# Finishing of a chunk's value sums, spread over more places of the loop

## The chip, the cores and the metric

The kernel runs on one core of one Trainium2 chip. The metric is the device time of one execution in microseconds (us). Engines are named as the profile names them: PE is TensorE (PEld its weight loads), DVE is VectorE, ACT is ScalarE, POOL is GpSimd, SP is SyncE.

## The reference: what is computed

For one sequence of 2048 rows and 512 features in float32 the result is `g * a + (1 - g) * b`. `g` is a sigmoid of a row sum. `b` is a SwiGLU network with 1792 hidden features. `a` is attention with 32 heads of 16 features in a sliding window of 256 keys:

```
scores = einsum("bhqd,bhkd->bhqk", q, k) * Dh ** -0.5
mask   = (i - j >= 0) & (i - j < 256)
p      = softmax(where(mask, scores, -1e9))
o      = einsum("bhqk,bhkd->bhqd", p, v)
a      = o.reshape(B, S, D) @ wo
```

The change lies in the last step of `o`: the sums over the keys are divided by the softmax's denominators and stored.

## The kernel before, in words

The 32 heads are worked on in 8 groups of four. A group's 2048 queries are 16 blocks of 128, and four blocks make a chunk of 512 queries. So there are 32 chunks in all.

The order of the work is written out by hand. The main loop, from L698, counts `t` from 0 to 128. Each `t` is one block of one group and has four steps, `hd` = 0 to 3, one for each head. Four values of `t`, `part` = 0 to 3, make a **slot** `d`: sixteen steps, one chunk. A pair (part, hd) names a step of a slot, and this document writes it (0,0) to (3,3). Engines take their instructions in the order in which the loop writes them, each engine in its own queue, and the framework adds a wait wherever one instruction touches data that another still uses.

Each step writes, in this order:

- `stage1` (L302, L304) for the next group: PE multiplies queries and keys into a PSUM tile `ps` of the pool `ps1`, and DVE adds the mask and takes the row maximum. The pool has two buffers, so the matmul of a step needs the DVE result of two steps before. The last group has no next group, so from t = 112 on there is no `stage1`.
- `stage2` (L344, L346, L348, L351) for this group: PE computes the transposed scores, ACT takes the exponential into `pt`, and POOL cuts two masks into `pt` once in two steps, at hd = 1 and hd = 3.
- three pairs of matmuls (L252) of the gate, up or projection products, which fill PE between the two stages.
- the functions put down in `AT` for this step, such as evictions, products, splits into high and low parts (`split`, L73, whose low part POOL computes) and DMAs.
- at some steps, one piece of `FIN`.

At (0,1), after everything else of the step, `av` (L356) writes the value products of the chunk that the previous slot has made ready: some 2 us of matmuls (L368) in which PE does nothing else. It leaves two PSUM tiles, `first` and `second`. The generator `finish` (L375) then turns them into stored results, one piece at each `run(FIN, 1)`. It uses two SBUF tiles of 128x512, `o0` and `o1`, which are called `both` and `ot` for even chunks; for odd chunks the names are swapped (L381). The pieces before the change, with the steps at which they are written:

- (0,1): ACT copies `second` to `both` (L383).
- (0,2): DVE adds `first` (L385, and L387 for a group's first chunk).
- (1,1): DVE transposes `both` into `ot` in 32x32 blocks (L389).
- (1,3): DVE takes the reciprocal of the denominators (L393) and multiplies all 512 columns' sums by it (L394).
- (2,1): DVE transposes `ot` back into `both` (L397), and POOL issues the DMA that stores `both` in `od` (L398).

After the loop the last phase begins: four matmul tiles of the SwiGLU part (L770), then the products with `wo`, which read `od`, and the down projection.

Of the kernel before, what the change touches and what calls it, by code (L numbers as in the profile page):

```python
# [12 lines left out]
ALU = mybir.AluOpType  # L13
# [3 lines left out]
P = 128  # L17
S, D, H, DH, W, F = 2048, 512, 32, 16, 256, 1792
NK = D // P
NB = S // P  # L20
CH = 512
# [15 lines left out]
def gated_mix(ctx, tc, xT, xn, wqk, wv, wo, wgu, wd, gw, outT):  # L37
# [4 lines left out]
    nc = tc.nc  # L42
# [51 lines left out]
    def run(gen, n=None):  # L94

        while n is None or n > 0:
            if next(gen, run) is run:
                break
            n = n and n - 1
# [101 lines left out]
    with ExitStack() as A:  # L201
# [88 lines left out]
        def stage1(g, qb):  # L290

            hf, b = divmod(qb, NB // 2)
            if b == 0:
                MX[g, hf] = sm.tile([P, 4, NB // 2], F32, name="mx")
            q0, k0 = qb * P, max(0, qb - 2) * P
            n = q0 + P - k0
            for hd in range(4):
                pr, j = divmod(hd, 2)
                r = slice(64 * j, 64 * j + 63)

                ps = ps2.tile([P, CH], F32, name="ps2") if g == 0 and pr else ps1.tile([P, CH], F32, name="ps1")
                nc.tensor.matmul(ps[:, :n], QT[g % 2][pr][r, q0:q0 + P], KT[g % 2][pr][r, k0:k0 + n],  # L302
                                 start=True, stop=True)
                mx = nc.vector.tensor_tensor_reduce(out=ps[:, :n], in0=ps[:, :n], in1=mask[:, 3 * P - n:],  # L304
                                                    scale=1.0, scalar=NEG, op0=ALU.add, op1=ALU.max,
                                                    accum_out=MX[g, hf][:, hd, b:b + 1])
                if g == 0:
                    BEHIND.append(mx)
                yield
# [18 lines left out]
        def load_v(n):  # L328

            VG[n] = sm.tile([P, 4, VW], F32, name="vg", bufs=4)  # L330
            nc.sync.dma_start(VG[n], vd[n // 4, :, n % 4 * 4:n % 4 * 4 + 4])

        def stage2(g, kb):


            n = min(3, NB - kb) * P
            k0 = kb * P
            for hd in (1, 0, 3, 2):
                pr, j = divmod(hd, 2)
                r = slice(64 * j, 64 * j + 64)  # L340
                if j:
                    pt = PT[g, kb, pr] = ptp.tile([P, 2, 3 * P], F32, name="pt")
                ps = ps2.tile([P, CH], F32, name="ps2")
                nc.tensor.matmul(ps[:, :n], KT[g % 2][pr][r, k0:k0 + P], QT[g % 2][pr][r, k0:k0 + n],  # L344
                                 start=True, stop=True)
                BEHIND.append(nc.scalar.activation(pt[:, j, :n], ps[:, :n], AF.Exp, scale=SCALE))  # L346
                if not j:
                    nc.gpsimd.affine_select(out=pt[:, :, :P], in_=pt[:, :, :P], pattern=[[0, 2], [1, P]],  # L348
                                            compare_op=ALU.is_ge, fill=0.0, base=0, channel_multiplier=-1)
                    if n == 3 * P:  # L350
                        nc.gpsimd.affine_select(out=pt[:, :, 2 * P:], in_=pt[:, :, 2 * P:],  # L351
                                                pattern=[[0, 2], [-1, P]], compare_op=ALU.is_ge, fill=0.0,
                                                base=-1, channel_multiplier=1)
                yield

        def av(g, c):  # L356


            AV[g, c] = (pp.tile([P, CH], F32, name="pb" if 4 * g + c + 1 < G * NB // 4 else "pa"),
                        ps1.tile([P, CH], F32, name="ps1") if 4 * g + c + 1 >= 4 * (G - 1) else ps2.tile([P, CH], F32, name="ps2"))  # L360

            todo = [(h, 4 * c + m) for h, m in SEQUENCE if 4 * c + m >= 0]
            at = [[n for n, (o, _) in enumerate(todo) if o == h] for h in range(2)]
            for n, (h, kb) in enumerate(todo):
                o, k0 = HALVES[h], kb * P + 64 * h
                q0, q1 = max(k0, c * CH), min(k0 + W + 64, c * CH + CH)
                for j in range(4):
                    nc.tensor.matmul(AV[g, c][h][32 * j:32 * j + 32, q0 - c * CH:q1 - c * CH],  # L368
                                     VG[4 * g + kb // 4][o, kb % 4, 17 * j:17 * j + 32],
                                     PT[g, kb, j // 2][o, j % 2, q0 - kb * P:q1 - kb * P],  # L370
                                     start=n == at[h][0], stop=n == at[h][-1], skip_group_check=True)
# [3 lines left out]
        def finish(g, c):  # L375


            first, second = AV[g, c]
            if not AB:
                AB.extend(osb.tile([P, CH], F32, name=f"o{n}") for n in range(2))  # L380
            both, ot = AB[::-1] if c % 2 else AB  # L381
            lo = 0 if c else 64
            nc.scalar.copy(both[:, lo:], second[:, lo:])  # L383
            yield
            nc.vector.tensor_tensor(out=both[:, lo:], in0=first[:, lo:], in1=both[:, lo:], op=ALU.add)  # L385
            if lo:
                nc.vector.tensor_copy(both[:, :lo], first[:, :lo])  # L387
            yield
            nc.vector.transpose(ot, both)  # L389
            yield  # L390
            v = ot.rearrange("p (s e) -> p s e", e=32)
            rc = osb.tile([P, CH // 32], F32, name="rc")
            nc.vector.reciprocal(rc, v[:, :, DH])  # L393
            nc.vector.tensor_tensor(out=v[:, :, :DH], in0=v[:, :, :DH],  # L394
                                    in1=rc[:, :, None].to_broadcast([P, CH // 32, DH]), op=ALU.mult)
            yield
            nc.vector.transpose(both, ot)  # L397
            nc.gpsimd.dma_start(od[g, :, c * CH:(c + 1) * CH], both)  # L398
            yield

# [142 lines left out]
        def later(t, hd, *fs):  # L543
            AT.setdefault((t, hd), []).extend(fs)
# [65 lines left out]
        def unit(t):  # L610

            def both(n, name):
                key, hf = TURNS[t // 2 + n]
                done = (group_half(t, key[1], hf) if key[0] == "p" else (gate_half, up_half)[key[2]](t, key[1], hf))
                two = []

                def turn(m):
                    if not two:
                        two.extend(lanes(pp, name, [products(key, 2 * hf + m) for m in range(2)], done))
                    yield from two[m]  # L620
                return turn(0), turn(1)
            (a0, a1), (b0, b1) = (both(n, name) for n, name in enumerate(("pa", "pb")))
            return [a0, b0, a1, b1]
# [55 lines left out]
        for b in range(NB):  # L679
            t, hd = blocks[b]  # L680
            later(t, hd, lambda b=b: gate_block(b))
            if b > 1:
                t, hd = blocks[b - 2]
# [10 lines left out]

        FIN = iter(())
        for t in range(G * NB + 1):  # L698
            g, i = divmod(t, NB)
            d, part = divmod(t, NSLOT)  # L700
            if part == 0:
                turns = unit(t) if t < G * NB else [iter(())] * NSLOT
            s1 = stage1(g + 1, i) if t < g7 else iter(())
            s2 = stage2(g, i) if t < G * NB else iter(())
            for hd in range(4):
                run(s1, 1)
                if t < g7:
                    run(s2, 1)
                elif hd % 2 == 0:
                    run(s2, 2)  # L710
                run(turns[part], 3)
                for f in AT.pop((t, hd), ()):
                    f()
                if (part, hd) in ((0, 2), (1, 1), (1, 3), (2, 1)):
                    run(FIN, 1)
                if hd == 1 and part == 0:
                    if t:
                        ag, c = divmod(d - 1, NCH)
                        av(ag, c)
                        FIN = finish(ag, c)  # L720
                        run(FIN, 1)
            if i in (7, 15) and g + 1 < G:
                later(t + 1, 2, lambda g=g, i=i: put_max(g + 1, i // 8))
            if t >= 10 and t % 4 == 2 and t + 6 < G * NB:
                load_v((t + 6) // 4)
        run(FIN)
        for key in sorted(AT):
# [4 lines left out]
    with ExitStack() as B:  # L732
# [7 lines left out]
        def column():  # L740
            return hp.tile([P, CH], F32, name="sg", bufs=4)
# [321 lines left out]
        two, t, part, rest = bank(4, 1), *(column() for _ in range(3))  # L1063
# [46 lines left out]
```

## Time and profile before

| | |
|---|---|
| median of three runs | 805.55 us (805.36 to 805.84) |
| the profiled execution's own time | 804.89 us |
| its span, first to last instruction | 803.2 us |
| busy: PE, PEld | 797.1 us (99%), 688.1 us (86%) |
| busy: DVE, ACT, POOL | 627.8 us (78%), 433.0 us (54%), 345.4 us (43%) |
| mean granted clock of TensorE | 0.999 |

The profile is of one execution. Its instructions are counted from the start of the span. Idle time of an engine ahead of a group of instructions is given with what ended it; a name such as "DVE mx L304" is the instruction that released the waiting one. The main loop's slots run from about 79 us to about 601 us, some 16.3 us each.

### The profile page before, as it was taken

What the parts mean: (1) busy time and instruction counts of PE and PEld (TensorE: products, weight loads), DVE (VectorE), ACT (ScalarE), POOL (GpSimd) and SP (SyncE); (2) the same over time, 40 slices, a digit from 0 to 9 for tenths busy, and PEclk for the clock granted to TensorE, in tenths of its full rate; (3) what the DMA queues carried; (4) which work ended last, traced back from release to release, by engine and by line L of the source; (5) the groups of instructions that cost most, each with busy time, mean ns of one, the idle gap of its engine ahead of it and who ended that gap; (6) DMA issues with size and microseconds to landing.
All of it is one profiled execution on the core that took longest, in us unless ns stands there. A gap on an engine that the chain in (4) does not pass through costs nothing.

```text
span 803.2 us, 21509 instructions
## 1 busy us (share of the span) xinstructions
PE 797.1 (99%) x8247; PEld 688.1 (86%) x8247; DVE 627.8 (78%) x1686; ACT 433.0 (54%) x883; POOL 345.4 (43%) x647
## 2 busy tenths in 40 slices
PE   9999999999999999999999999999999999999998
PEld 7888999889889889889988988888888888888886
DVE  6397787868887787878777878888675478899896
ACT  7412656665566566555666656645643235554642
POOL 7711546564545556544656454546740111000212
PEclk9999999999999999999999999999999999999999
DMA  8574514424252453351444516335637899728436
GB/s 300 168 219 144 141 68 131 128 97 143 68 159 78 117 167 97 114 159 53 138 115 129 151 44 201 130 102 173 202 100 234 263 345 316 292 62 272 93 53 105
DMA packets 62107, 121.88 MB, mean 152 GB/s; under 512 B 10868, under 2 KB 19828, under 8 KB 61748
## 3 DMA queue, kind: packets, MB, share of 16 engines
q1 hardware_dynamic: 54900, 99.27, 39.9%
q0 software_dynamic: 7104, 21.24, 9.0%
q8 instruction: 65, 1.06, 0.6%
q14 instruction: 38, 0.31, 0.1%
HBM read 55.97 MB, written 39.34 MB: 119 GB/s over the span
## 4 chain that ended last, share of the span: by engine, by line
PE 97%; DVE 2%; DMA 0%; SPq 0%; issue 0%; ACT 0%
PE pa L252 24%; PE pb L252 24%; PE ps L302 6%; PE ps L368 5%; PE ps L344 4%; PE ps L89 4%; PE ps L88 4%; PE ps L90 4%; PE pb L368 4%; PE pb L232 2%; PE pa L232 2%; PE pb L89 2%; PE pb L88 2%; PE pa L89 2%; PE pa L88 2%; PE pb L90 2%
## 5 line engine op out<-in xcount | busy, mean ns | idle before, releaser
L304 DVE CUSTOM_DVE_ANT_0 ps<-ps,mask 128x384 f32<-128x384 f32 (+2 forms) x512 | 268.7, 540 | 100.2 <-PE ps L344 51.1
L346 ACT ACTIVATE pt<-ps 128x384 f32<-128x384 f32 (+2 forms) x512 | 238.5, 475 | 130.7 <-PE ps L302 74.0
L348 POOL TENSOR_SCALAR_AFFINE_SELECT pt<-pt 128x256 f32<-128x256 f32 x256 | 108.4, 424 | 200.5 <-ACT pt L346 199.7
L344 PE MATMUL ps<-q,k 64*128 64x384 f32 (+2 forms) x512 | 161.7, 333 | 0.0
L302 PE MATMUL ps<-k,q 63*128 63x384 f32 (+2 forms) x512 | 159.6, 332 | 0.5 <-DVE mx L304 0.5
L252 PE MATMUL pb<-xhi,wh 64*128 64x512 f32 x512 | 116.7, 395 | 0.0
L252 PE MATMUL pb<-xlo,wh 64*128 64x512 f32 x512 | 115.3, 391 | 0.0
L252 PE MATMUL pb<-xhi,wl 64*128 64x512 f32 x512 | 115.2, 391 | 0.0
L252 PE MATMUL pa<-xhi,wh 64*128 64x512 f32 x512 | 113.9, 393 | 0.0
L252 PE MATMUL pa<-xlo,wh 64*128 64x512 f32 x512 | 112.8, 391 | 0.0
L252 PE MATMUL pa<-xhi,wl 64*128 64x512 f32 x512 | 112.6, 391 | 0.0
L302 PEld LDWEIGHTS ps<-k,q 63*128 63x128 f32 x512 | 88.7, 185 | 16.9 <-DVE mx L304 3.6
L351 POOL TENSOR_SCALAR_AFFINE_SELECT pt<-pt 128x256 f32<-128x256 f32 x224 | 100.3, 448 | 0.0
L344 PEld LDWEIGHTS ps<-q,k 64*128 64x128 f32 x512 | 90.8, 184 | 3.6 <-ACT pt L346 0.2
L368 PE MATMUL ps<-pt,vg 64*32 64x320 f32 (+4 forms) x1408 | 74.2, 346 | 0.0
L304 DVE DVE_READ_ACCUMULATOR2_ANT mx<- 128x1 f32 x512 | 71.6, 140 | 0.0
L368 PE MATMUL pb<-pt,vg 64*32 64x320 f32 (+2 forms) x1360 | 69.9, 349 | 0.0
L252 PEld LDWEIGHTS pb<-xhi,wh 64*128 64x128 f32 x512 | 61.6, 185 | 6.0 <-DVE o L385 0.4
L252 PEld LDWEIGHTS pb<-xhi,wl 64*128 64x128 f32 x512 | 61.8, 184 | 5.1
L252 PEld LDWEIGHTS pa<-xhi,wl 64*128 64x128 f32 x512 | 59.4, 184 | 5.9
L252 PEld LDWEIGHTS pa<-xhi,wh 64*128 64x128 f32 x512 | 59.7, 186 | 3.8
L252 PEld LDWEIGHTS pb<-xlo,wh 64*128 64x128 f32 x512 | 61.9, 185 | 0.3
(305 smaller groups left out, 1612.5 us busy)
## 6 DMA issues: line engine op xcount, KB each, us to landing
kept_h<-ev SPq DMA_DIRECT2D x52, 256.0 KB
od<-o POOLq DMA_DIRECT2D x32, 256.0 KB, 3.7
raw<-wgu SPq DMA_DIRECT2D x28, 256.0 KB
q<-xhi SPq DMA_DIRECT2D x56, 128.0 KB
k<-xhi SPq DMA_DIRECT2D x56, 128.0 KB
outT<-sg POOLq DMA_DIRECT2D x28, 256.0 KB, 4.5
vd<-vs POOLq DMA_DIRECT2D x8, 672.0 KB, 4.8
vg<-vd SPq DMA_DIRECT2D x32, 168.0 KB
```

Of the source, the lines that this page charges most:

```text
L88: nc.tensor.matmul(ps, lh, rh, start=start and i == 0, stop=False, skip_group_check=skip)
L89: nc.tensor.matmul(ps, lh, rl, start=False, stop=False, skip_group_check=skip)
L90: nc.tensor.matmul(ps, ll, rh, start=False, stop=stop and i == n - 1, skip_group_check=skip)
L232: nc.tensor.matmul(ps, w, x, start=n == 0, stop=n == len(todo) - 1)
L252: mm = nc.tensor.matmul(ps[me], w[r], x[r], start=not second and i == 0, stop=bool(second) and i == n - 1)
L302: nc.tensor.matmul(ps[:, :n], QT[g % 2][pr][r, q0:q0 + P], KT[g % 2][pr][r, k0:k0 + n], start=True, stop=True)
L304: mx = nc.vector.tensor_tensor_reduce(out=ps[:, :n], in0=ps[:, :n], in1=mask[:, 3 * P - n:], scale=1.0, scalar=NEG, op0=ALU.add, op1=ALU.m ...
L344: nc.tensor.matmul(ps[:, :n], KT[g % 2][pr][r, k0:k0 + P], QT[g % 2][pr][r, k0:k0 + n], start=True, stop=True)
L346: BEHIND.append(nc.scalar.activation(pt[:, j, :n], ps[:, :n], AF.Exp, scale=SCALE))
L348: nc.gpsimd.affine_select(out=pt[:, :, :P], in_=pt[:, :, :P], pattern=[[0, 2], [1, P]], compare_op=ALU.is_ge, fill=0.0, base=0, channel_mu ...
L351: nc.gpsimd.affine_select(out=pt[:, :, 2 * P:], in_=pt[:, :, 2 * P:], pattern=[[0, 2], [-1, P]], compare_op=ALU.is_ge, fill=0.0, base=-1, ...
L368: nc.tensor.matmul(AV[g, c][h][32 * j:32 * j + 32, q0 - c * CH:q1 - c * CH], VG[4 * g + kb // 4][o, kb % 4, 17 * j:17 * j + 32], PT[g, kb, ...
```

## The change

The reciprocal stays at (1,3), alone. The multiplication is cut into two halves of 256 columns each, at (2,0) and (2,2). The second transposition moves to (0,1) of the next slot, behind that slot's `av`, and the DMA that stores the chunk moves to (0,3) of the next slot. A second generator, `OLD`, holds the rest of the previous chunk's `finish` for this. At steps where both stand, `FIN` now comes ahead of the functions of `AT`, and `OLD` at (0,3) comes behind them. The tiles `o0` and `o1` and their swap are the same.

```
             nc.vector.reciprocal(rc, v[:, :, DH])
-            nc.vector.tensor_tensor(out=v[:, :, :DH], in0=v[:, :, :DH],
-                                    in1=rc[:, :, None].to_broadcast([P, CH // 32, DH]), op=ALU.mult)
             yield
+            for s in (slice(0, CH // 64), slice(CH // 64, CH // 32)):
+                nc.vector.tensor_tensor(out=v[:, s, :DH], in0=v[:, s, :DH],
+                                        in1=rc[:, s, None].to_broadcast([P, CH // 64, DH]), op=ALU.mult)
+                yield
             nc.vector.transpose(both, ot)
+            yield
             nc.gpsimd.dma_start(od[g, :, c * CH:(c + 1) * CH], both)
             yield
...
-        FIN = iter(())
+        FIN = OLD = iter(())
...
                 run(turns[part], 3)
+                if (part, hd) in ((0, 2), (1, 1), (1, 3), (2, 0), (2, 2)):
+                    run(FIN, 1)
                 for f in AT.pop((t, hd), ()):
                     f()
-                if (part, hd) in ((0, 2), (1, 1), (1, 3), (2, 1)):
-                    run(FIN, 1)
+                if (part, hd) == (0, 3):
+                    run(OLD)
                 if hd == 1 and part == 0:
                     if t:
                         ag, c = divmod(d - 1, NCH)
                         av(ag, c)
-                        FIN = finish(ag, c)
+                        OLD, FIN = FIN, finish(ag, c)
+                        run(OLD, 1)
                         run(FIN, 1)
```

## The prediction

> **What bounds the kernel now.** I read the page's busy times first, then what PE waits for, then the order of events on DVE, POOL and PE around one chunk's finishing.
>
> ```profile
> PE 797.1 (99%) x8247; PEld 688.1 (86%) x8247; DVE 627.8 (78%) x1686; ACT 433.0 (54%) x883; POOL 345.4 (43%) x647
> ```
>
> PE is the bound: 797.1 of 803.2 us. DVE matters only where it makes PE wait, and that is at the mask-and-maximum, L304. The groups of line 302, its matmul, say how much that costs today.
>
> ```profile
>   DVE mx L304: 4.1, 13
> ```
>
> PE stood idle ahead of L302 for 4.1 us in 13 places. That is the most that a smoother DVE could give back through this wait. The clearest place lies in the slot that begins at 191.4 us (timelines of DVE, POOL, PEld and PE):
>
> ```profile
> 201.35 1.15 DVE L394 TENSOR_TENSOR o<-o,rc 128x256 f32<-128x256 f32 x1
> 202.90 0.13 DVE L304 DVE_READ_ACCUMULATOR2_ANT mx<- 128x1 f32 x1
> ...
> 200.93 1.29 POOL L73 TENSOR_TENSOR xlo<-ev,xhi 128x512 fp32r<-128x512 f32 x1
> ...
> 203.09 0.18 PEld L302 LDWEIGHTS ps<-k,q 63*128 63x128 f32 x1 [0.66 <-DVE mx L304]
> ...
> 201.14 0.45 PE L252 MATMUL pa<-xhi,wh 64*128 64x512 f32 x2
> 202.00 0.40 PE L252 MATMUL pa<-xhi,wh 64*128 64x512 f32 x2
> 203.31 0.45 PE L252 MATMUL pa<-xhi,wh 64*128 64x512 f32 x2
> ```
>
> The multiplication takes 1.15 us there, while a POOL subtraction runs beside it. The maximum comes late, the weight load of L302 waits 0.66 us, and the step from 202.00 to 203.31 takes 1.31 us where the one before it took 0.86. So such a collision costs PE about 0.45 us. The rows also give two latencies that I need below: L304's last part ended at 203.03, the weight load started 0.06 us later, and the step's L252 came 0.22 us after that.
>
> **The change part by part.** One whole chunk in the middle shows what is there:
>
> ```profile
> 314.13 0.71 DVE L389 STREAM_TRANSPOSE o<-o 128x512 f32<-128x512 f32 x1
> 314.76 0.53 DVE L304 CUSTOM_DVE_ANT_0 ps<-ps,mask 128x384 f32<-128x384 f32 x1
> 315.21 0.13 DVE L304 DVE_READ_ACCUMULATOR2_ANT mx<- 128x1 f32 x1
> ...
> 315.87 0.25 DVE L393 RECIPROCAL rc<-o 128x16 f32<-128x16 f32 x1
> 316.15 0.51 DVE L394 TENSOR_TENSOR o<-o,rc 128x256 f32<-128x256 f32 x1
> ...
> 310.83 0.57 DVE L304 CUSTOM_DVE_ANT_0 ps<-ps,mask 128x384 f32<-128x384 f32 x1 [2.86 <-PE ps L344]
> ...
> 318.61 0.56 POOL L398 DMA_DIRECT2D od<-o  x1
> ```
>
> *The multiplication in halves.* The 0.51 us at (1,3) becomes two instructions at (2,0) and (2,2). The trace has no half; each costs between 0.25 and 0.51 us, and I take 0.3. Both lie beside PE's step of 0.87 us. If that cover were gone, they would add 0.1 us to a slot. The gain is bounded by 0 and the 4.1 us above. I count two collisions like the one shown, 0.9 us.
>
> *The second transposition at (0,1).* It costs the same 0.71 us, but DVE stands idle for 2.86 us there, while PE does the value products. It is free, and ACT's copy L383 behind it waits for those products anyway.
>
> *The DMA at (0,3) of the next slot.* This is the part that costs. In the code of before, chunk c stores from `both`, and chunk c+1 uses that same tile as its `ot`: the first transposition L389 overwrites it. So L389 must wait until the store of the chunk before has landed. Today the store is issued at 318.61 and the next L389 comes 13 steps later, some 12 us. After the change the store is written at (0,3) and L389 at (1,1), two steps later. How long a store takes (groups of line 398, issue to landing):
>
> ```profile
> L398 POOL DMA_DIRECT2D od<-o x32: 560/560/584, 105.0 to 604.8; - x32
> ...
> DMA to landing us min/median/max: 2.3/3.7/7.7
> ```
>
> No store of 32 landed in less than 2.3 us, and two steps are 1.75 us. Queued behind L389 on DVE is L304 of step (1,2), for which L302 of step (2,0) waits, and with it all of PE. I work it out at three of the slots, the first that is hit, one in the middle, and the last. The rows are POOL's last mask cut of step (0,3), behind which the store will stand; L389; the end of L304 of step (1,2); and PE's first L252 of step (2,0). For the middle slot the second and third stand above.
>
> ```profile
> 115.95 0.41 POOL L351 TENSOR_SCALAR_AFFINE_SELECT pt<-pt 128x256 f32<-128x256 f32 x1
> ...
> 117.53 0.71 DVE L389 STREAM_TRANSPOSE o<-o 128x512 f32<-128x512 f32 x1
> ...
> 118.61 0.14 DVE L304 DVE_READ_ACCUMULATOR2_ANT mx<- 128x1 f32 x1
> ...
> 119.11 0.45 PE L252 MATMUL pa<-xhi,wh 64*128 64x512 f32 x2
> ...
> 312.83 0.41 POOL L351 TENSOR_SCALAR_AFFINE_SELECT pt<-pt 128x256 f32<-128x256 f32 x1
> ...
> 315.88 0.39 PE L252 MATMUL pa<-xhi,wh 64*128 64x512 f32 x1
> ...
> 526.89 0.41 POOL L351 TENSOR_SCALAR_AFFINE_SELECT pt<-pt 128x256 f32<-128x256 f32 x1
> ...
> 528.10 0.71 DVE L389 STREAM_TRANSPOSE o<-o 128x512 f32<-128x512 f32 x1
> ...
> 529.19 0.13 DVE L304 DVE_READ_ACCUMULATOR2_ANT mx<- 128x1 f32 x1
> ...
> 529.97 0.44 PE L252 MATMUL pa<-xhi,wh 64*128 64x512 f32 x2
> ```
>
> Middle slot: the cut ends at 313.24, the store is issued at about 313.27 and lands 2.3 us later at 315.57 at best. L389 starts 0.06 us after that, at 315.63 instead of 314.13, so 1.50 us late. L304 then ends at 316.84 instead of 315.34, and the L252 follows 0.06 + 0.22 us behind, at 317.12 instead of 315.88: PE loses 1.24 us. In the same way the first slot loses 1.14 us and the last 1.21. The mean is 1.2 us with a store at its fastest; every further microsecond of the store is one more for PE.
>
> *How many slots.* The first chunk has no store ahead of it. The slots of the last group have no L304 that could hold PE:
>
> ```profile
> L304 DVE CUSTOM_DVE_ANT_0 ps<-ps,mask x512: 288/566/601, 37.6 to 536.8; 128x384 f32<-128x384 f32 x150, 128x128 f32<-128x128 f32 x11, 128x256 f32<-128x256 f32 x10
> ```
>
> Its last instruction stands at 536.8 us, so 26 of the 32 transpositions count, those from 117.53 to 528.10. 26 x 1.2 = **31.2 us**. The other five I take at nothing, since PE's matmuls of the same slots cover the late DVE work; without that cover they would cost 5 x 1.2 = 6 us.
>
> *Whether the store has the DMA engines to itself.* For each of the 26 slots I took the stretch in which the new store would move its bytes, 1.1 to 2.0 us after its issue, and read the share of the DMA engines that other transfers take there today. In 16 of them it is 0.11 or less, in 10 it is 0.24 to 1.00. The first and the last of either kind:
>
> ```profile
> 117.49:118.39 0.90, 0.90 (x12) 0.90 (x10) 0.90 (x4) 0.49 (x1) 0.70 (x2) 1.00 0.03 9
> 528.43:529.33 0.90, 0.90 (x12) 0.76 (x10) 0.90 (x4) 0.49 (x1) 0.61 (x2) 1.00 0.00 0
> ...
> 134.22:135.12 0.90, 0.90 (x12) 0.78 (x10) 0.86 (x4) 0.52 (x2) 0.51 (x2) 1.00 0.78 191
> 494.88:495.78 0.90, 0.90 (x12) 0.85 (x10) 0.89 (x3) 0.49 (x1) 0.62 (x2) 1.00 1.00 370
> ```
>
> A free store takes 2.3 us. For a shared one I take 3.0, half way to the median of 3.7: 10 x 0.7 = **7.0 us**. The bounds are 0 (all at 2.3) and 26 x 1.4 = 36.4 us (all at the median).
>
> The Trainium skill gives a formula in its page "DMA: Bandwidth & Descriptors", section "Anatomy of one DMA — SWDGE (gpsimd) path": about 2.0 us fixed and the bytes at 436 GB/s. An estimate by it is 2.6 us for 256 KB; all 26 slots at that would add 26 x 0.3 = 8 us to the 31.2 in place of my 7.0. The row's least value lies below it and its median above, so the trace agrees only between the two.
>
> *What stands ahead of the store on POOL.* At (0,3) the functions of `AT` come first. In three slots one of them is a POOL subtraction of an `xlo`, which today follows right behind the last mask cut of (0,3):
>
> ```profile
> 198.44 1.81 POOL L73 TENSOR_TENSOR xlo<-ev,xhi 128x512 fp32r<-128x512 f32 x1
> ...
> 329.84 1.80 POOL L73 TENSOR_TENSOR xlo<-ev,xhi 128x512 fp32r<-128x512 f32 x1
> ...
> 461.28 1.30 POOL L73 TENSOR_TENSOR xlo<-ev,xhi 128x512 fp32r<-128x512 f32 x1
> ```
>
> It delays the store by its own length. I take the shorter, 1.3 us, because DVE will be waiting beside it: 3 x 1.3 = **3.9 us**. POOL itself, past which the DMA moves, gains nothing for PE: its mask cuts now stand behind an issue at (0,3) instead of (2,1), 0.56 us either way, while POOL has idle time in every slot.
>
> *The end.* The last chunk's transposition waits for the store of the one before it, at most some 3 us. PE then works on four SwiGLU tiles that need nothing of it. I take 0, with 3 us as the bound.
>
> The sum: 31.2 + 7.0 + 3.9 - 0.9 = 41.2 us. Against the profiled execution's own time that is 804.89 + 41.2 = 846.1 us. The median of the runs lies 0.66 us above the profiled execution, so I forecast 847 us.
>
> **The rivals.**
>
> *The store lands in time.* This is the case that isn't slower. If a store landed within about 1.1 us of its issue (2.3 less the 1.2 us that PE loses), or if L389 had nothing to wait for, PE would lose nothing and keep the gain: 804.9 - 0.9 = 804.0, down to 800.8 with all of the 4.1 us. Against it stands the least landing of 2.3 us in 32, and that the two tiles alternate by chunk and no third one is added. Chance 0.03.
>
> *PE's clock falls while it waits.* The end of the trace shows that an idle PE loses its clock (stretches of time, granted clock in the column after POOL):
>
> ```profile
> 799.00:800.00 1.00, 0.18 (x2) 0.00 (x0) 0.96 (x3) 0.00 (x0) 0.00 (x0) 1.00 0.64 250
> ...
> 801.00:802.00 1.00, 0.00 (x0) 0.00 (x0) 0.00 (x0) 0.00 (x0) 0.00 (x0) 0.90 0.36 124
> 802.00:803.20 1.20, 0.00 (x0) 0.00 (x0) 0.00 (x0) 0.00 (x0) 0.00 (x0) 0.50 0.00 0
> ```
>
> PE's last matmul ends near 799.2, and the clock goes to 0.50 near 801.8, 2.6 us later. Stalls of 1.2 us repeated once a slot are shorter, but those behind a shared store or a POOL subtraction come near. If each stall cost as long at half clock as the fall took, 2.6 us, PE would lose 1.3 us more in each: 26 x 1.3 = 34, and the time would be 881 us. Chance 0.05. The Trainium skill's page "TensorE: Matmul & The Clock Gate", section on the HAM clock gate, says that the clock halves after an idle window of about 3.4 us and returns after as long a busy one; an estimate by that page is 1.7 us a stall and 891 us if every stall triggered it, and nothing if none does, since none of mine is that long. The 2.6 us of the trace are in its range, since the page lets the windows run free.
>
> *Every store is shared.* The stores now all leave at one place of the slot, and the SP queue's transfers may move towards them as the slots get longer. Then all 26 take the median: 31.2 + 36.4 + 3.9 - 0.9 = 70.6, 876 us. For it speaks the median of today; against it the 16 free stretches. Chance 0.10.
>
> *PE loses only half.* If in a stalled slot POOL's mask cut of (0,3) came earlier against DVE, the stall would shrink; at half of it the time is 804.9 + 20.6 = 826 us. Against it: POOL's cuts follow ACT's exponentials, which follow PE, and so does L389. Chance 0.05.
>
> **How the numbers follow.** My forecast has 0.76. The five chances leave 0.01 for anything else. A change of under 0.2% can't be told from none here. Slower by more is every case but the first: 0.96. Faster by over 0.2% needs more than 1.6 us of gain with no stall: 0.02. Within: 0.02. The range runs from 828 us (all stores at 2.3 us, no delay on POOL, all of the 4.1 us gained is 832, and some of the half-loss case) to 877 us (every store at the median). It leaves out the clock, the landing in time and half of the half loss, about 0.12.
>
> **What would show it.** On DVE, idle time ahead of L389 with the store as its releaser, 1.5 us or more in each of the 26 slots; PE idle ahead of L302 of step (2,0), released by L304, some 40 us in all; the steps (2,0) 1.2 us longer. The transposition L397 in DVE's gap during the value products, with no wait behind it. The 0.45 us losses behind L394 gone. I am wrong if L389 starts on time, if PE's loss sits elsewhere, or if the granted clock falls below 0.99.

## The result

The changed kernel takes 864.92 us (863.69 to 866.82, four runs); the kernel before took 805.45 us in the same comparison (805.11 to 805.84). The ratio is 1.074, with a 95% interval of 1.073 to 1.075. So it is 59.5 us slower. The forecast was 847 us, in a range of 828 to 877: the direction and the wait behind it hold, the size came out 18 us larger, and a second mechanism, PE's clock, took a part that the forecast had put at nothing. The figures of the experiments below leave out one execution of 1119.07 us, in which the granted clock was 0.655.

The page of the changed kernel, busy times, and two of its costliest groups (busy, mean ns of one, then idle time ahead of the group and what ended it):

```profile
PE 818.0 (95%) x8247; PEld 694.5 (80%) x8247; DVE 632.0 (73%) x1718; ACT 432.2 (50%) x883; POOL 337.9 (39%) x647
...
L302 PE MATMUL ps<-k,q 63*128 63x384 f32 (+2 forms) x512 | 165.0, 342 | 39.9 <-DVE mx L304 39.9
...
L389 DVE STREAM_TRANSPOSE o<-o 128x512 f32<-128x512 f32 x32 | 22.8, 711 | 57.8 <-DMA od<-o 57.8
```

Before, PE was busy for 99% of its span; now it is 95% of a longer one. DVE stands idle for 57.8 us ahead of L389, always until a store of `od` has landed, where before it never waited there. PE stands idle for 39.9 us ahead of L302 until DVE's maximum L304.

The slot that the prediction worked out in the middle of the loop now looks like this (timelines of DVE, POOL, PEld and PE):

```profile
340.34 0.14 DVE L304 DVE_READ_ACCUMULATOR2_ANT mx<- 128x1 f32 x1
342.39 0.71 DVE L389 STREAM_TRANSPOSE o<-o 128x512 f32<-128x512 f32 x1 [1.91 <-DMA od<-o]
343.02 0.53 DVE L304 CUSTOM_DVE_ANT_0 ps<-ps,mask 128x384 f32<-128x384 f32 x1
343.48 0.13 DVE L304 DVE_READ_ACCUMULATOR2_ANT mx<- 128x1 f32 x1
...
339.58 0.56 POOL L401 DMA_DIRECT2D od<-o  x1
...
343.66 0.18 PEld L302 LDWEIGHTS ps<-k,q 63*128 63x128 f32 x1 [1.84 <-DVE mx L304]
...
341.39 0.41 PE L252 MATMUL pb<-xhi,wh 64*128 64x512 f32 x2
343.95 0.39 PE L252 MATMUL pa<-xhi,wh 64*128 64x512 f32 x2
```

The store is issued at 339.58, behind the mask cuts of step (0,3). DVE is done with step (1,1) at 340.48 and waits 1.91 us, until 342.39. L304 of step (1,2) ends at 343.61, the weight load of L302 follows 0.05 us later, and PE's step from 341.39 to 343.95 takes 2.56 us instead of 0.87. This is the chain that the prediction wrote down, instruction by instruction; only this slot's store took 2.8 us and not 2.3.

Where the 61.9 us between the two profiled spans went, from the starts of PE's steps in the two traces:

| part | us |
|---|---|
| the loop's first slot begins later | 1.0 |
| step (1,3) of the slots 2 to 27, behind L389 | 47.6 |
| steps behind it in the same slots, at half clock | 11.2 |
| other differences of these slots, the collisions' gain among them | -1.3 |
| last group, slots 28 to 30 | 3.3 |

The second part was forecast as 31.2 + 7.0 + 3.9 = 42.1 us. The third stood only in a rival. It is seen best in one slot (stretches of time, their length, the busy time of PE, PEld, DVE, ACT and POOL, then the granted clock, the DMA share and GB/s), and in PE's first L252 of its next steps:

```profile
241.80:245.20 3.40, 3.40 (x36) 2.92 (x34) 2.82 (x9) 1.93 (x4) 2.02 (x5) 1.00 0.33 131
245.20:248.60 3.40, 0.98 (x10) 0.50 (x6) 0.67 (x2) 0.53 (x2) 0.76 (x2) 1.00 0.42 134
248.60:252.00 3.40, 2.80 (x14) 2.69 (x16) 2.34 (x10) 0.86 (x2) 0.00 (x0) 0.51 0.00 0
252.00:255.50 3.50, 3.50 (x20) 3.31 (x20) 1.61 (x7) 1.10 (x3) 0.82 (x3) 0.51 0.00 0
255.50:258.90 3.40, 3.40 (x34) 3.30 (x32) 2.89 (x9) 2.88 (x7) 1.69 (x3) 1.00 0.00 0
...
249.69 0.70 PE L252 MATMUL pa<-xhi,wh 64*128 64x512 f32 x2
251.29 0.70 PE L252 MATMUL pa<-xhi,wh 64*128 64x512 f32 x2
```

From 245.2 to 248.6 PE works for 0.98 us of 3.40, and then the clock is half until 255.5. The steps take 1.60 us (249.69 to 251.29) instead of 0.87. The slots 2 to 27 have seven such falls, five of 3.4 us and two of 6.8 us, 30.7 us in all; one more lies in the last group.

The Trainium skill, page "TensorE: Matmul & The Clock Gate", section "Part 1: The HAM clock gate (the "warmup" mystery)", describes a free-running window of about 3.4 us; the distances between the falls in this trace are whole multiples of 3.41 us, so that agrees. It says that the clock halves after an idle window. Here a part of a window was enough: ahead of the seven falls PE stood idle for 1.91 to 2.75 us of the window, and no window of the slots 2 to 27 with 1.73 us or less began one.

### The profile page after: what moved, and what is told of

Read it like the earlier page. It is cut to its first block, busy times and chain, and to the rows that moved or that the text cites. A ratio compares the mean times of both kernels' runs of the same rounds, so it can differ in the third digit from the quotient of the medians.

```text
span 865.1 us, 21536 instructions
## 1 busy us (share of the span) xinstructions
PE 818.0 (95%) x8247; PEld 694.5 (80%) x8247; DVE 632.0 (73%) x1718; ACT 432.2 (50%) x883; POOL 337.9 (39%) x647
## 4 chain that ended last, share of the span: by engine, by line
PE 77%; DMA 10%; DVE 4%; POOL 3%; ACT 3%; issue 2%; SPq 0%; POOLq 0%; ACTq 0%; DVEq 0%
PE pa L252 21%; PE pb L252 14%; DMA od<-o 8%; PE ps L302 6%; PE ps L368 4%; PE ps L88 4%; PE ps L89 4%; PE ps L90 4%; PE pb L368 3%; PE ps L344 3%; DVE o L389 2%; ACT pt L346 2%; PE pb L232 2%; PE pa L89 2%; PE pb L88 2%
## 5 line engine op out<-in xcount | busy, mean ns | idle before, releaser
L304 DVE CUSTOM_DVE_ANT_0 ps<-ps,mask 128x384 f32<-128x384 f32 (+2 forms) x512 | 269.9, 542 | 105.6 <-PE ps L302 55.7
L348 POOL TENSOR_SCALAR_AFFINE_SELECT pt<-pt 128x256 f32<-128x256 f32 x256 | 107.7, 421 | 267.6 <-ACT pt L346 267.1
L302 PE MATMUL ps<-k,q 63*128 63x384 f32 (+2 forms) x512 | 165.0, 342 | 39.9 <-DVE mx L304 39.9
L344 PE MATMUL ps<-q,k 64*128 64x384 f32 (+2 forms) x512 | 167.1, 344 | 1.4 <-ACT pt L346 1.4
L302 PEld LDWEIGHTS ps<-k,q 63*128 63x128 f32 x512 | 91.3, 190 | 65.2 <-DVE mx L304 52.2
L252 PE MATMUL pa<-xhi,wh 64*128 64x512 f32 x512 | 115.4, 411 | 0.0
L252 PE MATMUL pa<-xlo,wh 64*128 64x512 f32 x512 | 114.2, 408 | 0.0
L252 PE MATMUL pa<-xhi,wl 64*128 64x512 f32 x512 | 113.6, 406 | 0.0
L252 PE MATMUL pb<-xhi,wh 64*128 64x512 f32 x512 | 110.5, 394 | 0.0
L252 PE MATMUL pb<-xlo,wh 64*128 64x512 f32 x512 | 109.1, 391 | 0.0
L252 PE MATMUL pb<-xhi,wl 64*128 64x512 f32 x512 | 109.1, 391 | 0.0
L344 PEld LDWEIGHTS ps<-q,k 64*128 64x128 f32 x512 | 93.7, 189 | 7.1 <-ACT pt L346 2.7
L351 POOL TENSOR_SCALAR_AFFINE_SELECT pt<-pt 128x256 f32<-128x256 f32 x224 | 93.8, 419 | 0.0
L304 DVE DVE_READ_ACCUMULATOR2_ANT mx<- 128x1 f32 x512 | 71.9, 140 | 0.0
L389 DVE STREAM_TRANSPOSE o<-o 128x512 f32<-128x512 f32 x32 | 22.8, 711 | 57.8 <-DMA od<-o 57.8
L252 PEld LDWEIGHTS pa<-xhi,wl 64*128 64x128 f32 x512 | 59.3, 195 | 6.7
L252 PEld LDWEIGHTS pa<-xhi,wh 64*128 64x128 f32 x512 | 59.0, 195 | 4.1
L252 PEld LDWEIGHTS pb<-xhi,wh 64*128 64x128 f32 x512 | 56.0, 186 | 5.9
L252 PEld LDWEIGHTS pb<-xhi,wl 64*128 64x128 f32 x512 | 56.0, 184 | 5.9
```

Of the source, the lines that this page charges most:

```text
L252: mm = nc.tensor.matmul(ps[me], w[r], x[r], start=not second and i == 0, stop=bool(second) and i == n - 1)
```

## The experiments

Each kernel is given as a diff against the changed kernel, unless the text says otherwise; `...` marks lines left out.

### The store two written steps earlier

```
-            yield
             nc.gpsimd.dma_start(od[g, :, c * CH:(c + 1) * CH], both)
```

> The changed kernel with one yield taken out: the store of a chunk is issued at (0,1), right behind the transposition L397, and not two written steps later at (0,3). Everything else is as changed. Theory (the whole loss is L389 waiting at (1,1) for that store, and what PE and its clock lose by it): the store now has the value products' 2.2 us more, lands near 311 in a slot where L389 starts at 314, the wait vanishes, the granted clock is 0.998 or more, and the time is 804 us (803 to 806). Rival (the transposition at (0,1), the halves, or the new order against the other functions of a step cost something of their own): it stays above 815 us with DVE or ACT as the releaser.

Measured: 815.09 us, ratio 1.0125 (1.0102 to 1.0149), granted clock 0.999. Idle time ahead of L389, and ahead of L302 (here the waits of its weight load, 11.8 us, and of its matmul, 7.2 us, are added):

```profile
  DMA od<-o: 17.1, 12
...
  DVE mx L304: 18.9, 22
```

One line takes 50 of the 59.5 us away, but not all of it, so the number was missed by 11 us. L389 still waits in 12 slots, longest 5.4 us (after the loop's last chunk, where it holds no L304). In those of the slots 2 to 27 the store landed only 3.5 to 6.0 us after its issue, and in four of them it also left some 3 us behind the transposition, because POOL had mask cuts and subtractions (L73) to do first; step (1,3) still loses 9.6 us over the slots 2 to 27. The releaser is the same store, not DVE or ACT as the rival had it.

### The store alone moved

The diff is against the kernel before.

```
             nc.vector.transpose(both, ot)
+            yield
             nc.gpsimd.dma_start(od[g, :, c * CH:(c + 1) * CH], both)
...
+                if (part, hd) == (0, 3):
+                    run(OLD)
...
-                        FIN = finish(ag, c)
+                        OLD, FIN = FIN, finish(ag, c)
```

> The kernel before with one part of the change alone: the multiplication stays whole at (1,3), the second transposition stays at (2,1) of its own slot, and only the store moves to (0,3) of the next slot. Theory: the same wait of L389 for the same store, so the same loss: 47 us in the steps behind (1,3), some 11 us of steps at half clock, 3 us in the last group, 864 us (855 to 872). Rival (the loss needs the transposition or the halves in their new places): under 830 us.

Measured: 866.50 us, ratio 1.074 (1.072 to 1.077), granted clock 0.984.

```profile
  DMA od<-o: 67.2, 31
```

With the multiplication whole and the transposition in its old place, the place of the store alone makes the whole loss: 46.5 us at (1,3), 11.0 us at half clock. The other two parts of the change neither cause it nor soften it. The last group loses 3.5 us, near the 3 expected: 1.7 in the slots 28 to 30 and 1.7 in the last slot. Here L389 waits up to 4.8 us in these slots, and what stands behind it on DVE, such as the products L572, then makes PE wait by up to 1.0 us.

### The first transposition one step later, and one earlier

```
-                if (part, hd) in ((0, 2), (1, 1), (1, 3), (2, 0), (2, 2)):
+                if (part, hd) in ((0, 2), (1, 2), (1, 3), (2, 0), (2, 2)):
```

> The changed kernel with the first transposition L389 one step later, at (1,2) and not (1,1). Theory: each stall is shorter by one step of 0.87 us; from the 26 stalls of the changed kernel, each less 0.87 and none below zero, 25 us are left, with 3 us in the last group and 3 to 5 falls of the clock at 1.7 us each: 840 us (832 to 848). Rival (the stall is a fixed cost of the new order, whatever the distance): 855 us or more.

The other kernel has (1, 0) in that place.

> The changed kernel with L389 one step earlier, at (1,0). Theory: 0.87 us more in each of 26 slots, 22.7 us, and a granted clock below the changed kernel's 0.979, since more stalls pass some 1.9 us of idle PE within one window of the clock gate: 10 to 15 falls, 895 us (886 to 908). Rival (the clock has no part in the loss): 887 us at 0.979 or above, the 22.7 us alone.

Measured: 842.72 us at (1,2), ratio 1.0455 (1.0441 to 1.0468), clock 0.990; 914.36 us at (1,0), ratio 1.136 (1.133 to 1.139), clock 0.951. Idle time ahead of L389, first at (1,2), then at (1,0):

```profile
  DMA od<-o: 41.4, 30
```

```profile
  DMA od<-o: 78.1, 30
```

The stall follows the distance between store and transposition. The stalled step, over the slots 2 to 27, loses 28.9 us at (1,2), 47.6 us at (1,1) and 74.0 us at (1,0). The time grows faster than that: 22.2 us for the first step and 49.4 us for the second. The rest is the clock. The time at half clock in the slots 2 to 27 is 17.1, 30.7 and 85.3 us in the three traces, and the steps behind the stall lose 8.1, 11.2 and 33.7 us. The number for (1,0) was missed by 19 us: 22 falls and not 10 to 15. Stalls long enough to halve the clock are dearer than their own length.

### The store ahead of the step's other functions

```
+                if (part, hd) == (0, 3):
+                    run(OLD)
                 for f in AT.pop((t, hd), ()):
                     f()
-                if (part, hd) == (0, 3):
-                    run(OLD)
```

> The changed kernel with the store at (0,3) written ahead of the other functions of that step, not behind them. Theory: in the three slots where POOL first works on an xlo (the ones around 199, 330 and 461 us of the kernel before) the store leaves 1.3 to 1.8 us earlier; their stalls go from 3.1 to 3.3 us to some 1.7, and two falls of the clock with them, 1.8 us: 4.5 to 6.5 us less than the changed kernel, 859 us (856 to 862). Rival (POOL's place in the queue doesn't matter, since the transfers set the landing): 863 us or more.

Measured: 853.32 us, ratio 1.0595 (1.0571 to 1.0618), clock 0.992, 11.6 us less than the changed kernel.

```profile
  DMA od<-o: 53.8, 30
```

The three slots with an `xlo` on POOL lose 1.1, 1.2 and 1.1 us at (1,3) now, after 3.3, 3.1 and 3.3. That is 6.4 us, more than the 3.9 us that the forecast gave them: the stores leave 1.8, 1.8 and 1.3 us earlier in their slots, and they also land faster, in 2.3 to 2.4 us after 2.5 to 3.3. The rival falls. Three falls of the clock are left of seven in the slots 2 to 27, and the steps at half clock cost 4.3 us instead of 11.2. Not all of that belongs to the edit. Two of the falls that are gone, worth 4.2 us, stood in slots 9 and 11, where the stall is nearly as long as before (3.2 and 3.0 us after 3.5 and 3.0). Their idle time now falls across two windows of the clock, 1.4 and 1.5 us in slot 9, 1.5 and 1.2 us in slot 11. That part of the gain is luck with the position of the windows, and it is the main reason why the gain is larger than expected.

### A third tile

```
-EV = 5
+EV = 4
...
-                AB.extend(osb.tile([P, CH], F32, name=f"o{n}") for n in range(2))
-            both, ot = AB[::-1] if c % 2 else AB
+                AB.extend(osb.tile([P, CH], F32, name=f"o{n}") for n in range(3))
+            both, ot = AB[(4 * g + c) % 3], AB[(4 * g + c + 1) % 3]
```

> The changed kernel with a third tile in the rotation: chunk n uses tile n mod 3 as both and the next one as ot, so L389 writes a tile that no store is reading. For the room, the pool of the evicted products (ev) has 4 buffers in place of 5. Everything stays where the change put it, the store at (0,3) and L389 at (1,1). Theory: no wait of L389 for a store, granted clock 0.998 or more; the loss is gone but for what 4 ev buffers cost: 804 to 815 us. Rival (the loss is in the new places and not in the shared tile): 855 us or more.

Measured: 812.05 us, ratio 1.0085 (1.0071 to 1.0099). PE's group of L302:

```profile
L302 PE MATMUL ps<-k,q 63*128 63x384 f32 (+2 forms) x512 | 159.0, 331 | 1.0 <-DVE mx L304 1.0
```

L389 never waits for a store. The slots 2 to 27 are 1.1 us shorter than in the kernel before, with the store at (0,3) and L389 at (1,1) as the change has them. All that is left, 9.1 us, lies in the last group. ACT's tanh (L571) waits there 4.3 and 3.2 us for a store of `kept_h` out of an `ev` buffer, PE waits 3.3 and 2.1 us behind it, and the clock falls twice. The smaller pool would explain it, as the expectation says; no run has the smaller pool alone, and with five buffers the changed kernel already loses 1.5 us in the first of these slots. So the shared tile is the cause in the slots 2 to 27.

### The store at (0,1) and the first transposition at (1,3)

```
-            yield
             nc.gpsimd.dma_start(od[g, :, c * CH:(c + 1) * CH], both)
...
-                if (part, hd) in ((0, 2), (1, 1), (1, 3), (2, 0), (2, 2)):
+                if (part, hd) in ((0, 2), (1, 3), (2, 0), (2, 1), (2, 3)):
```

> As store_at_01 (the store at (0,1), behind L397), and the first transposition two steps later, at (1,3), with the reciprocal at (2,0) and the halves at (2,1) and (2,3). With the store at (0,1) alone 9 us were left, in the 12 slots where L389 still waited, up to 1.7 us of PE each. Theory: two steps are 1.75 us, so no wait of L389 holds PE any more; the two 0.5 us losses behind the whole multiplication stay gone; the last group may keep some 2 us: 804 to 807 us. Rival (the 9 us are a cost of the transposition or the halves in their places): 811 us or more.

Measured: 806.1 us, ratio 1.0005 (0.9996 to 1.0014). A second run of the same kernel has the trace:

> The same kernel as store_01_transp_13, for a trace of it: 806.5 us again. Theory: up to the last group it is some 1 to 2.5 us ahead of the kernel before (the collisions behind L394 are gone, no stall at L302 in their place), and it loses about 2 us in the last group's first slot, where the row maximum's negation (L315) now stands behind the transposition L399 and the addition L385 on DVE: SP's md, wd and kept_h transfers leave 1.1 us later there and a tanh waits for the kept_h store. Rival: the loss of that slot is not there, and small stalls are spread over all slots.

Measured: 805.64 us, ratio 0.9998 (0.9989 to 1.0008). The whole loss is gone, and nothing is won. The trace shows both halves of the expectation. The slots 2 to 27 are 1.8 us shorter; in two of them the 0.5 us behind the whole multiplication are gone. The last group is 1.9 us longer, 1.2 us of it in its first slot. There SP issues the row maxima (`md`) at this time, first in the kernel before and then in this one:

```profile
542.61 0.58 SPq L318 DMA_DIRECT2D md<-mtt  x1
```

```profile
542.65 0.58 SPq L318 DMA_DIRECT2D md<-mtt  x1
```

The slot begins at 537.1 us in the first and at 535.8 us in the second, so `md` leaves 5.5 us into the slot before, and 6.9 us now. DVE does four block sums there, and ahead of L315, the negation of the row maximum, now stand the transposition L399 and the addition L385, which itself waits 0.7 us for ACT's copy; two casts stood ahead of it before too. The transfers in SP's queue behind `md` are as late, and a tanh on ACT waits 2.0 us for one of them, a store of `kept_h`, where it waited 0.2 us before.

### The same with FIN behind the other functions

The diff is against the kernel of the section above.

```
-                if (part, hd) in ((0, 2), (1, 3), (2, 0), (2, 1), (2, 3)):
-                    run(FIN, 1)
                 for f in AT.pop((t, hd), ()):
                     f()
+                if (part, hd) in ((0, 2), (1, 3), (2, 0), (2, 1), (2, 3)):
+                    run(FIN, 1)
```

> As store_01_transp_13, and the pieces of FIN stand behind the other functions of their step again, as before the change; only OLD's transposition stays ahead. Theory: in the last group's first slot L315 is no longer behind the addition L385 (0.6 us), SP's transfers leave earlier, and the 1.9 us there shrink to under 1: 804.5 us (803.3 to 805.8), 1 to 2 us ahead of store_01_transp_13. Rival (the order against the other functions has no part): 806 us or more.

Measured: 806.75 us, ratio 1.0012 (1.0004 to 1.0021).

```profile
541.82 0.58 SPq L318 DMA_DIRECT2D md<-mtt  x1
```

The slot begins at 536.2 us, so `md` is back at 5.6 us, and the slot's loss falls from 1.2 us to 0.1. That step of the reasoning holds. The time does not: it is 1.1 us more than its neighbour, where 1 to 2 us less were expected. The profiled execution, 805.14 us, is the fastest of the eleven runs, and its trace does not hold what makes the others slower. This is left open.

### The halves in their own slot

Both kernels are the kernel before with the multiplication cut in two, as in the change, and nothing crosses into the next slot. The first has the second transposition and the store at (3,1); of its diff against the kernel before, the places are:

```
-                if (part, hd) in ((0, 2), (1, 1), (1, 3), (2, 1)):
+                if (part, hd) in ((0, 2), (1, 1), (1, 3), (2, 0), (2, 2), (3, 1)):
```

> The kernel before with the multiplication in halves at (2,0) and (2,2), and the second transposition with its store at (3,1) of the same slot; nothing crosses into the next slot. Theory: the store has 8 steps and the value products until the next L389, so no wait; the two collisions behind L394 go, 1.0 us: 804.5 us (803.5 to 806). Rival (the halves themselves cost PE time): over 808 us.

Measured: 813.46 us, ratio 1.0098 (1.0085 to 1.0112), a miss of 9 us. DVE in one slot:

```profile
190.35 0.69 DVE L573 SCALAR_TENSOR_TENSOR ev<-ev,pa 128x512 f32<-128x512 f32 x1
190.96 0.56 DVE L304 CUSTOM_DVE_ANT_0 ps<-ps,mask 128x384 f32<-128x384 f32 x1
...
191.44 0.68 DVE L573 SCALAR_TENSOR_TENSOR ev<-ev,pa 128x512 f32<-128x512 f32 x1
192.03 0.71 DVE L399 STREAM_TRANSPOSE o<-o 128x512 f32<-128x512 f32 x1
192.66 0.54 DVE L304 CUSTOM_DVE_ANT_0 ps<-ps,mask 128x384 f32<-128x384 f32 x1
```

Two products and a transposition, 2.1 us, stand in two steps beside two maxima. L304 comes late there, L302 waits for it, and PE loses 0.3 to 0.6 us at (3,3) in 20 slots, 9.3 us over the slots 2 to 27. The two collisions did go, 0.5 us each.

The second has the reciprocal at (1,2), the halves at (1,3) and (2,0), and the transposition with its store at (2,1) as before. Against the first:

```
-                if (part, hd) in ((0, 2), (1, 1), (1, 3), (2, 0), (2, 2), (3, 1)):
+                if (part, hd) in ((0, 2), (1, 1), (1, 2), (1, 3), (2, 0), (2, 1)):
```

> The kernel before with the finishing spread inside its own slot only: reciprocal at (1,2), halves at (1,3) and (2,0), the second transposition and the store at (2,1) as before. Halves_only lost 0.4 to 0.6 us in 17 slots at (3,3), because its second transposition at (3,1) stood in the same two steps as the two products L571 on DVE. Theory: with the transposition back at (2,1) that loss is gone, and the two collisions of 0.5 us as well: 804.5 us (803.5 to 805.5). Rival (halves cost PE time wherever they stand): over 807 us.

Measured: 805.33 us, ratio 0.9995 (0.9986 to 1.0003). The loss at (3,3) is gone, so it was the place of the transposition. The collisions are back in part: of the 0.5 us only 0.1 is won at (2,1), and as much is lost at (2,3). No kernel here beats the one before by more than the measurement can tell.

## Why the prediction was right, and where it was not

**The wait, its place and its releaser: right.** "L389 must wait until the store of the chunk before has landed": L389 starts 0.02 us after the landing in every one of the 26 slots. "Queued behind L389 on DVE is L304 of step (1,2), for which L302 of step (2,0) waits": PE's loss stands in exactly that step. The third tile shows that the shared tile is the cause in these slots, and the store moved alone that nothing else is needed.

**26 x 1.2 = 31.2 us at the fastest store, and 7.0 us for sharing: too small by some 5 us.** The 16 slots that were read as free had stores of 2.6 us in the mean (2.3 to 3.7), the 10 that were read as shared 3.2 us (2.3 to 5.1), against 2.3 and 3.0 forecast. The sum of the differences is 16 x 0.25 + 10 x 0.2, about 6 us. The stalled steps' 47.6 us divide into 13.4 us for what the stores took beyond 2.3 us each, 4.8 us for the later issue in the three slots with an `xlo`, and 29.4 us, or 1.13 a slot, that even the fastest store costs. So 1.2 a slot was nearly right, and the term that was too small is the 7.0 us. The store's landing after the change:

```profile
DMA to landing us min/median/max: 2.3/2.6/7.3
```

So the new place really is quieter than the old one, whose median was 3.7, and the rival in which every store is shared falls. What was missed were above all three stores of 4.1 to 5.1 us, which made stalls of 3.0 to 4.4 us; they are half of the 13.4 us. The reading of today's transfers did not sort the slots well: three of the ten that were read as shared had stores of under 2.5 us, and two of the sixteen that were read as free had 3.3 and 3.7 us.

**The three `xlo` on POOL, 3.9 us: right in kind, too small.** They delayed the issue by 4.8 us, since two of the three subtractions took 1.8 us and not the 1.3 that was chosen. Taking them away shortened the three stalls by 6.4 us, the rest through stores that land faster.

**PE's clock, a rival at 0.05: the part that failed.** The step said that "stalls of 1.2 us repeated once a slot are shorter" than the 2.6 us after which the clock fell at the end of the trace. That holds for the short ones. But it made the clock an affair of all 26 stalls or of none, and put nothing of it into the sum, though it named the slots that "come near". Seven stalls were long enough, and their falls cost 11.2 us in the steps behind them. The 2.6 us were the time from PE's end to the fall, not the least idle time that brings one: 1.91 us within a window did. The trace of before already spoke against a whole idle window: the fall came 2.6 us after PE's last matmul, so PE was still at work in the first 0.8 us of the 3.41 ahead of it. The prediction held that windows that run free allow for this; but a window of 3.41 us that is idle from end to end cannot close 2.6 us after PE's last matmul. The prediction had itself named the sign, "or if the granted clock falls below 0.99": it was 0.979. The profiled execution lies 20.7 us above the 846.1 of the sum; 11.2 of that are the clock in the slots 2 to 27, 5.5 the stalled steps and 3.3 the last group.

**The last group, taken at nothing with 6 us as the bound: 3.3 us.** The cover that was named, PE's matmuls, did hold: L389 waits 0.2 to 0.8 us in the slots 29 to 31, and PE's steps behind it are no longer than before. (With the store alone moved it waits up to 4.8 us there, and the cover does not hold.) The loss comes from elsewhere.

```profile
612.26 0.44 PE L344 MATMUL ps<-q,k 64*128 64x384 f32 x1 [1.39 <-ACT pt L346]
...
613.90:617.30 3.40, 3.40 (x46) 1.58 (x50) 2.32 (x5) 0.00 (x0) 0.66 (x2) 0.50 0.04 17
```

In slot 28, where L389 does not wait at all, `md` leaves 6.9 us into the slot and not 5.5, a tanh on ACT waits 2.2 us for a store of `kept_h`, and PE waits 1.39 us for the exponential behind it; the slot is 1.5 us longer. DVE's new order at (0,1) and (0,2) makes the small DMA late, and SP's queue behind it; `store_01_13_behind` supports that by giving 1.1 us of that slot back. Then the clock falls at 613.9 us and makes the value products of slot 29 1.6 us longer. The forecast counted each moved step on its own engine and on POOL's queue, and not what stood behind it on SP's.

**The end, taken at 0: right.** The last chunk's L389 waits 4.7 us, more than the 3 us named as the bound, and what follows the loop's last step takes as long as before within 0.1 us.

**The gain, 0.9 us: about right in size, worth nothing.** The bound of 4.1 us was misread: that row adds the waits of L302's weight load, 3.6 us, and of its matmul, 0.5 us. The two collisions were 0.5 us each, and where no stall covers them they vanish with the halves at the new places. Kernels that keep this and lose the wait come out level with the kernel before.

**The free place for L397, in DVE's idle time during the value products: right** for the 26 slots. Only in the last group's first slot, where the block sums fill DVE, it was not free.

## What to carry to other kernels

When a store is moved later, look for the next writer of the tile it reads, count the steps between them, and compare that with the shortest landing in the trace; two tiles that swap roles are enough only while the store has a good part of a round to land. A wait in an engine's queue is paid by whatever stands behind it, and an instruction that makes a DMA late is paid by SP's queue too. And price a stall of PE with its clock: the losses here grew from 22 to 49 us for the same 0.87 us more in each slot, once the stalls filled more than half of a clock window.

## What the runs showed of the hardware that was not expected

PE's clock halves on a fixed grid of 3.41 us. In the slots 2 to 27 of the changed kernel the windows ahead of a fall held 1.91 to 2.75 us of idle PE, and those with up to 1.73 us did not bring one; with L389 at (1,2) the limit lay below 2.0 us as well, and in the kernel with the store alone moved between 1.80 and 1.95. With L389 at (1,0), where falls follow each other closely, single ones began at 1.73 to 1.79 us, while other windows with 1.56 to 1.78 us brought none; so the limit is not sharp. In these kernels a fall lasted one window where PE was idle for up to 0.44 us of it, and two where it was idle for 0.56 to 1.99 us. Behind the slots 2 to 27 three falls came at less: in the last group of the changed kernel at 1.39 us of idle time, with L389 at (1,0) at 1.53 us, and in `store_ahead` at 1.63 us. What is different there is left open. The idle times rest on the matmuls' ends as the profile models them.

A store of 256 KB issued by POOL landed in 2.3 us at best in every kernel, and an L389 that waited for it started 0.02 to 0.10 us after, in the changed kernel's slots 2 to 27 always 0.02 us.
